# Row steps moved from VectorE to GpSimd, gate split moved to ScalarE and GpSimd, an early exp table, 65-column AV matmuls and a new order of the attention steps

## The chip, the cores and the metric

The kernel runs on one core of a Trainium2 chip. The metric is the device time of one execution in microseconds; the time of a kernel is the median of its runs.

## The reference

Attention over four batches with eight heads, 768 tokens and 64 dimensions, in which a query sees only the keys that were given the same of 16 centroids; then a layer of eight experts in which each token goes to one expert, by a greedy choice over all logits with a capacity of 384 tokens.

```python
q_assign = np.argmax(np.einsum('bhsd,hcd->bhsc', q_n, c_n), axis=-1)
k_assign = np.argmax(np.einsum('bhsd,hcd->bhsc', k_n, c_n), axis=-1)
mask = q_assign[:, :, :, None] == k_assign[:, :, None, :]
scores = scale * np.matmul(q, k.transpose(0, 1, 3, 2))
scores = np.where(mask, scores, -1000000000.0)
scores = scores - np.max(scores, axis=-1, keepdims=True)
attn = np.exp(scores)
attn = attn / (np.sum(attn, axis=-1, keepdims=True) + 1e-09)
out = np.matmul(attn, v)
...
for e in range(E):
    h = np.maximum(x[mask_e] @ w1[e], 0.0)
    out[mask_e] = h @ w2[e]
```

## The kernel before

**Units.** The attention is cut into eight units u (a batch and one half of its heads: four heads). Of each head there are six blocks of 128 queries and six of 128 keys. All operands are split into a high and a low f16 part, so that products are close to f32.

**Steps of a unit.** The kernel is written as named steps, and the string `ATT_ORDER` lists all of them in one order for the whole attention; the listed order is the program order on every engine, and no scheduler changes it. `load` brings q, k or v in, `split_sc`, `split_hi` (ScalarE) and `split_lo` (GpSimd for units 0 and 1, VectorE else) make the parts, `trans` or `pt`/`ptc` turn them around, `cent` and `hot0` to `hot5` find the centroid of each token. Then, 24 times each per unit:

- `m_mm` (TensorE, L765) computes the masked scores of one query block against all keys, and `m_rd` (VectorE, L769) takes the row maximum from PSUM;
- `b_mm` (TensorE, L804 and L808) computes the scores turned around, with the row maximum as additional rows of the operand, and `b_exp` (ScalarE, L811) the exponential;
- `res` (GpSimd, L819, tile `rt`; 12 of the 192 on VectorE) makes the low part of the exponential;
- `av` (TensorE, L830 to L836) multiplies with v: for each of six query blocks three matmuls, with 66, 64 and 66 columns, into the accumulator `av` in PSUM; one `av` in six has six more of 66 columns.

After the six `av` of a head, `out0`, `out1`, `out2`, `hi0` and `hi1` divide by the sum and split the result.

**Row steps.** When the 12 maxima of one half of a unit are there (six, one head, in unit 0), `row0` (L787) and `row1` (L783) make two small f16 tables from them on VectorE. `rowt` and `row2` are two DMAs on SyncE's queue that bring these tables into `qbt`, which the `b_mm` of that half read. `m_mm` of a later unit are listed between, so that TensorE has other work until then. `m_mm` and `b_mm` share three PSUM tiles `sc`.

**Around it.** `wgs` (`gate_split`, L547 and L548) splits the gate's weights on VectorE. The matmuls that form the logits (`lg0`) read them. `wd` (`dummy`, L655) is a matmul of 384 columns whose result nobody reads; there are 91, all in the first 46 us. `c1` takes square roots on ScalarE, and `b_exp` exponentials; ScalarE loads a table of functions before the first of each. `tab` steps fill tables that the second part needs. The second part, from 400 us on, is the routing and the experts (`FFN_ORDER`).

Of the kernel before, what the change touches and what calls it, by code (L numbers as in the profile page):

```python
# [25 lines left out]
hh3,0 hh4,0,k hh4,0,q split_sc,0,q,1 split_hi,0,q,1,P split_lo,0,q,1,P pt,0,qa,1 load,0,k,1 split_sc,0,k,1 split_hi,0,k,1,P
split_lo,0,k,1,P pt,0,ka,1 ptc,0,ka,1,D wd load,0,q,3 split_sc,0,q,3 split_hi,0,q,3,P split_lo,0,q,3,P load,0,k,3
split_sc,0,k,3 load,0,k,2 split_sc,0,k,2 wd wd wd wd load,0,v,- wd wd hh5,0,k split_sc,0,v,- wd wd zqb tab,4 cent0,1,k
ptc,0,qa,1,D ptc,0,qa,2,D tab,7 hh5,0,q cent0,1,q hh0,1 hh1,1 tab,2 pt,0,qa,3 pt,0,kb,0 split_hi,0,v,-,P ptc,0,kb,0,D
pt,0,qb,0 ptc,0,qb,0,A ptc,0,qa,3,D wd wd split_hi,0,k,3,P dup,0,k,3 hh2,1 hh3,1 wd dup,0,q,1 hh4,1,q load,1,v,- hh4,1,k  # L30
dup,0,k,1 hh5,1,q hh5,1,k wd wd wd wd tab,22 wd m_mm,0,1 m_rd,0,1 m_mm,0,0 wd wd wd wd wd split_hi,0,k,2,P dup,0,k,2
m_rd,0,0 m_mm,0,2 m_rd,0,2 wd wd pt,0,qb,1 ptc,0,qb,1,D dup,0,q,2 m_mm,0,4 m_rd,0,4 split_lo,0,v,-,P vs,0 split_lo,0,k,3,P
load,1,k,- split_sc,1,k,- pt,0,ka,3 ptc,0,ka,3,D split_lo,0,k,2,P pt,0,ka,2 tab,24 vh2,0 vact,0 tab,5 ptc,0,ka,2,A vl2,0
m_mm,0,5 m_rd,0,5 split_hi,1,k,-,P wd wd wd pt,0,kb,1 cent0,2,k cent0,2,q hh0,2 hh1,2 hh2,2 tab,8 hh3,2 hh4,2,q hh4,2,k wd
wd wd wd wd wd wd wd m_mm,0,3 m_rd,0,3 wd wd wd wd tab,23 ptc,0,kb,1,A m_mm,0,6 m_rd,0,6 cent0,3,k cent0,3,q hh0,3 row1,0,0
hh1,3 hh2,3 load,1,q,- wd row0,0,0 hh5,2,q tab,20 wd m_mm,0,8 pt,0,qb,2 wd wd dup,0,q,3 hh3,3 m_rd,0,8 m_mm,0,7 hh5,2,k
hh4,3,k hh4,3,q split_sc,1,q,- split_hi,1,q,-,P split_lo,1,k,-,P wd wd wd wd wd wd wd ptc,0,qb,2,A wd trans,1,ka,- m_rd,0,7
m_mm,0,10 m_rd,0,10 hh5,3,q hh5,3,k split_sc,1,v,- split_hi,1,v,-,P wd wd wd wd wd wd pt,0,kb,3 ptc,0,kb,3,D pt,0,kb,2
dup,1,k,- m_mm,0,11 wd ptc,0,kb,2,D wd wd m_mm,0,9 m_rd,0,11 cent,1,k,0 cent,1,k,3 cent,1,k,1 cent,1,k,2 split_lo,1,q,-,P
m_rd,0,9 hot0,1,k hot1,1,k pt,0,qm,0 row0,0,1 hot2,1,k ptc,0,qm,0,A pt,0,qb,3 ptc,0,qb,3,A m_mm,0,15 tab,34 m_rd,0,15  # L40
hot3,1,k row1,0,1 wd wd trans,1,qa,- wd b_mm,0,0 wd b_exp,0,0 res,0,0,P dup,1,q,- wd wd m_mm,0,12 hot4,1,k hot5,1,k
m_rd,0,12 wd wd m_mm,0,13 m_rd,0,13 m_mm,0,14 m_rd,0,14 cent,1,q,0 cent,1,q,3 cent,1,q,1 cent,1,q,2 hot0,1,q hot1,1,q
load,2,k,- pt,0,qm,1 trans,1,kb,- ptc,0,qm,1,A hot2,1,q wd wd split_lo,1,v,-,P b_mm,0,1 b_exp,0,1 res,0,1,P b_mm,0,2
b_exp,0,2 b_mm,0,3 wd wd wd hot3,1,q hot4,1,q b_exp,0,3 res,0,3,P m_mm,0,17 m_rd,0,17 m_mm,0,16 m_rd,0,16 tab,1 wd tab,16
hot5,1,q trans,1,qb,- m_mm,0,18 split_hi,2,k,-,D av,0,0 tab,17 row0,0,2 dup,2,k,- m_mm,0,22 row1,0,2 m_rd,0,18 vs,1
m_rd,0,22 tab,27 pt,0,qm,2 ptc,0,qm,2,A m_mm,0,19 vact,1 av,0,1 b_mm,0,4 m_rd,0,19 res,0,2,P b_exp,0,4 res,0,4,P b_mm,0,5
b_exp,0,5 split_lo,2,k,-,D tab,25 vh2,1 res,0,5,P load,2,q,- b_mm,0,6 b_exp,0,6 res,0,6,P vl2,1 m_mm,0,20 m_rd,0,20 tab,14
av,0,2 b_mm,0,7 b_exp,0,7 m_mm,0,21 m_rd,0,21 av,0,3 m_mm,1,0 m_rd,1,0 b_mm,0,9 b_exp,0,9 res,0,9,P m_mm,0,23 m_rd,0,23
row1,0,3 av,0,4 loadg row0,0,3 m_mm,1,1 m_rd,1,1 b_mm,0,8 b_exp,0,8 m_mm,1,2 m_rd,1,2 av,0,5 pt,0,qm,3 load,3,q,-
ptc,0,qm,3,A tab,30 res,0,8,P out0,0,0 b_mm,0,10 b_exp,0,10 wgs out1,0,0 out2,0,0,D m_mm,1,3 hi0,0,0 m_rd,1,3 b_mm,0,12  # L50
b_exp,0,12 b_mm,0,11 b_exp,0,11 m_mm,1,4 hi1,0,0 m_rd,1,4 split_hi,2,q,-,D av,0,6 m_mm,1,5 m_rd,1,5 b_mm,0,13 b_exp,0,13
res,0,7,P tab,6 av,0,7 av,0,8 split_lo,2,q,-,D res,0,10,P b_mm,0,14 b_exp,0,14 load,2,v,- m_mm,1,7 m_rd,1,7 m_mm,1,6
m_rd,1,6 res,0,11,P av,0,9 load,3,k,- av,0,10 m_mm,1,13 m_rd,1,13 split_hi,2,v,-,D res,0,13,P av,0,11 out0,0,1 res,0,12,P
out1,0,1 out2,0,1,D b_mm,0,15 m_mm,1,8 m_rd,1,8 m_mm,1,11 m_rd,1,11 trans,2,ka,- tab,21 cent,2,k,0 cent,2,k,1 cent,2,k,2
b_exp,0,15 trans,2,qa,- m_mm,1,10 m_rd,1,10 hi0,0,1 res,0,14,P hi1,0,1 b_mm,0,17 b_exp,0,17 cent,2,k,3 hot0,2,k res,0,15,P
b_mm,0,18 hot1,2,k m_mm,1,9 res,0,17,P m_rd,1,9 tab,3 tab,32 row1,1,0 b_exp,0,18 b_mm,0,16 b_exp,0,16 xst,0,0 row0,1,0
tab,26 av,0,12 av,0,13 av,0,14 hot2,2,k hot3,2,k split_hi,3,k,-,D split_lo,3,k,-,D b_mm,0,19 b_exp,0,19 b_mm,0,20 hot4,2,k
av,0,15 b_exp,0,20 hot5,2,k res,0,16,P av,0,16 av,0,17 out0,0,2 m_mm,1,14 m_rd,1,14 b_mm,0,21 b_exp,0,21 out1,0,2 out2,0,2,D
b_mm,0,22 b_exp,0,22 xtr,0,0 lg0,0,0 lg1,0,0 res,0,18,P m_mm,1,12 m_rd,1,12 hi0,0,2 res,0,19,P hi1,0,2 b_mm,0,23 m_mm,1,18
cent,2,q,0 m_rd,1,18 b_exp,0,23 cent,2,q,3 m_mm,1,15 m_rd,1,15 res,0,22,P rowt,1,0 res,0,20,P row2,1,0 b_mm,1,1 b_exp,1,1  # L60
m_mm,1,19 trans,2,kb,- cent,2,q,2 dup,2,q,- split_hi,3,q,-,D cent,2,q,1 m_mm,1,16 m_rd,1,19 m_rd,1,16 m_mm,1,17 hot0,2,q
m_rd,1,17 av,0,18 b_mm,1,3 av,0,19 res,0,23,P b_mm,1,2 b_exp,1,3 b_exp,1,2 hot1,2,q b_mm,1,0 av,0,20 b_exp,1,0 hot2,2,q
hot3,2,q hot4,2,q hot5,2,q trans,3,ka,- res,0,21,P av,0,21 res,1,1,P b_mm,1,5 b_exp,1,5 res,1,5,P m_mm,1,21 load,4,q,-
split_lo,2,v,-,D m_rd,1,21 av,0,22 av,0,23 out0,0,3 tab,36 m_mm,1,20 res,1,2,P m_rd,1,20 b_mm,1,6 b_exp,1,6 out1,0,3
out2,0,3,D hi0,0,3 m_mm,1,23 trans,2,qb,- vs,2 vact,2 res,1,0,P m_mm,1,22 b_mm,1,4 b_exp,1,4 m_rd,1,23 res,1,4,P b_mm,1,7
b_exp,1,7 hi1,0,3 m_rd,1,22 row1,1,1 av,1,0 res,1,3,P b_mm,1,8 b_exp,1,8 row0,1,1 rowt,1,1 vh2,2 m_mm,2,1 av,1,1
split_lo,3,q,-,D m_rd,2,1 m_mm,2,3 av,1,2 vl2,2 m_mm,2,0 xst,0,1 b_mm,1,10 b_exp,1,10 av,1,3 m_rd,2,3 av,1,4 res,1,6,P
load,3,v,- m_rd,2,0 row2,1,1 m_mm,2,2 m_rd,2,2 av,1,5 out0,1,0 tab,18 res,1,8,P cent,3,k,0 out1,1,0 out2,1,0,D m_mm,2,4
b_mm,1,11 m_rd,2,4 b_exp,1,11 m_mm,2,5 cent,3,k,2 xtr,0,1 res,1,10,P hi0,1,0 m_rd,2,5 hi1,1,0 cent,3,k,1 cent,3,k,3
res,1,7,P hot0,3,k hot1,3,k b_mm,1,9 b_exp,1,9 res,1,9,P m_mm,2,7 m_rd,2,7 m_mm,2,8 load,4,k,- tab,28 m_rd,2,8 av,1,6  # L70
b_mm,1,12 tab,10 b_exp,1,12 av,1,7 res,1,11,P av,1,8 av,1,9 hot2,3,k hot3,3,k dup,3,k,- b_mm,1,14 b_exp,1,14 hot4,3,k
hot5,3,k res,1,12,P res,1,14,P tab,33 av,1,10 av,1,11 trans,3,qa,- b_mm,1,13 m_mm,2,6 out0,1,1 out1,1,1 b_exp,1,13
res,1,13,P out2,1,1,D hi0,1,1 m_rd,2,6 b_mm,1,17 b_exp,1,17 res,1,17,P b_mm,1,15 b_exp,1,15 hi1,1,1 xtr,1,0 lg0,0,1 lg1,0,1
lg2,0,1 m_mm,2,9 m_rd,2,9 m_mm,2,14 m_rd,2,14 b_mm,1,16 load,4,v,- m_mm,2,11 m_rd,2,11 av,1,12 res,1,15,P b_exp,1,16
m_mm,2,10 xst,1,0 m_rd,2,10 av,1,13 m_mm,2,13 m_rd,2,13 m_mm,2,12 m_rd,2,12 row1,2,0 row0,2,0 rowt,2,0 av,1,14
# [1394 lines left out]
```

## Time and profile before

| | us |
|---|---|
| median of 3 runs (lowest to highest) | 704.22 (703.09 to 706.07) |
| the profiled execution | 704.8 |
| its span, first to last instruction | 703.0 |
| TensorE busy in the span | 659.1 |
| VectorE busy | 522.7 |
| GpSimd busy | 497.2 |
| ScalarE busy | 424.0 |
| mean granted clock of TensorE | 0.968 |

Matmuls are pipelined: a busy time of TensorE holds the latency of each, so that what it could take is read from the distance between starts. The attention lies in the first 400 us. The share of an engine is read there by stretches, not over the whole span.

### The profile page before, as it was taken

Reading aid. Unit: us, or ns where it says so; the run is one execution under the profiler, and the core shown is the slowest. Engines: PE = TensorE matmul, PEld = TensorE weight load, DVE = VectorE, ACT = ScalarE, POOL = GpSimd, SP = SyncE. Lnnn points to the kernel's source line nnn. Section 1 sums busy time; section 2 is a strip of 40 time slices with the busy share of each in tenths; the row PEclk is TensorE's granted clock in tenths of the full one; section 3 lists DMA queues with packets and bytes.
Section 4 is the critical chain, followed back from the end, with each engine's and each line's share of the span. In section 5 each row is a group of like instructions: output and inputs, shape, how many; then the busy total and the mean of one; then the engine's idle time right before and its main releaser. Section 6 shows DMA issues by size and latency. Waiting matters only on the chain. (4 is left out here: it accounts for less than half of the span.)

```text
span 703.0 us, 19737 instructions
## 1 busy us (share of the span) xinstructions
PE 659.1 (94%) x8274; PEld 438.3 (62%) x8274; DVE 522.7 (74%) x1149; ACT 424.0 (60%) x554; POOL 497.2 (71%) x395
## 2 busy tenths in 40 slices
PE   7988999969999999999998778999999999999996
...
DVE  6999989998899999987887867868676666742020
...
PEclk9999999998999999999999958999999999999998
...
GB/s 199 124 181 221 94 182 183 173 171 115 109 192 183 155 121 167 119 82 120 62 35 48 70 24 263 137 195 277 108 320 106 284 134 242 173 324 238 37 9 45
DMA packets 175450, 105.84 MB, mean 151 GB/s; under 512 B 135426, under 2 KB 160002, under 8 KB 175362
## 3 DMA queue, kind: packets, MB, share of 16 engines
...
q14 instruction: 24, 0.20, 0.1%
HBM read 58.77 MB, written 12.58 MB: 101 GB/s over the span
## 5 line engine op out<-in xcount | busy, mean ns | idle before, releaser
L819 POOL TENSOR_TENSOR rt<-pt 128x768 f16<-128x768 f32 x180 | 277.7, 1569 | 74.6 <-ACT pt L811 70.4
L811 ACT ACTIVATE pt<-sc 128x768 f32<-128x768 f32 x192 | 150.9, 811 | 114.3 <-PE sc L808 99.2
L769 DVE TENSOR_REDUCE mxs<-sc 128x1 f32<-128x768 f32 x192 | 177.0, 949 | 19.9 <-PE sc L765 18.8
L1392 PE MATMUL pf<-xgt,w1h 128*128 128x384 f16 (+1 forms) x640 | 129.0, 293 | 0.2 <-DVE xgt L729 0.2
L830 PE MATMUL av<-vh,pt 128*128 128x66 f16 x1152 | 123.5, 195 | 3.5 <-DVE xb L863 3.5
L833 PE MATMUL av<-vh,rt 128*128 128x66 f16 x1152 | 123.2, 195 | 0.6 <-POOL rt L819 0.6
L832 PE MATMUL av<-vl,pt 128*128 128x64 f16 x1152 | 123.2, 193 | 0.0
L832 PEld LDWEIGHTS <-pt 128*128 128x128 bf16 x1152 | 107.3, 99 | 11.3 <-issue 4.6
L830 PEld LDWEIGHTS <-pt 128*128 128x128 bf16 x1152 | 107.8, 99 | 8.9 <-DVE xb L863 1.0
L833 PEld LDWEIGHTS <-rt 128*128 128x128 f16 x1152 | 106.8, 98 | 0.7 <-POOL rt L819 0.7
L765 PE MATMUL sc<-kbt,qbt 80*128 80x384 f16 x384 | 91.8, 330 | 11.0 <-DVE mxs L769 9.1
L804 PE MATMUL sc<-qbt,kbt 99*128 99x384 f16 x384 | 95.4, 329 | 3.3 <-DVE mxs L769 1.8
L808 PE MATMUL sc<-qat,kat 128*128 128x384 f16 x384 | 95.5, 330 | 0.0
L1392 PE MATMUL pf<-xgt,w1l 128*128 128x384 f16 (+1 forms) x320 | 90.0, 294 | 0.0
L1354 ACT ACTIVATE wr<-wr 128x1024 f32<-128x1024 f32 x64 | 66.7, 1046 | 24.6 <-DMA wr<-in_moe_w_dram 24.6
L1392 PEld LDWEIGHTS <-w1h 128*128 128x128 f16 x640 | 57.2, 97 | 29.1 <-issue 1.5
L1430 PE MATMUL pf<-w2h,hh 128*128 128x512 f16 x192 | 72.7, 378 | 0.0
L1430 PE MATMUL pf<-w2h,hl 128*128 128x512 f16 x192 | 72.6, 378 | 0.0
L1430 PE MATMUL pf<-w2l,hh 128*128 128x512 f16 x192 | 72.6, 378 | 0.0
L1368 POOL DMA_INDIRECT xg<-xrow,idx x24 | 23.3, 969 | 65.3 <-DVE idx L1327 33.8
L1364 POOL TENSOR_TENSOR w2l<-wr,w2h 128x1024 f16<-128x1024 f32 x32 | 67.7, 2136 | 1.4 <-ACT w2h L1357 1.0
L1364 POOL TENSOR_TENSOR w1l<-wr,w1h 128x1024 f16<-128x1024 f32 x32 | 67.3, 2130 | 0.2
...
## 6 DMA issues: line engine op xcount, KB each, us to landing
...
xg<-xrow,idx POOLq DMA_INDIRECT x24, 6.2
```

Of the source, the lines that this page charges most:

```text
L765: nc.tensor.matmul(p[:, half, :S // 2], QBT[u][:D + C, i, :], KBT[u][:D + C, h * J + half * 3:h * J + half * 3 + 3, :], start=True, stop=True)
L769: nc.vector.tensor_reduce(mxs[u % 3][:, i:i + 1], MP.pop((u, i))[:, :, :S // 2], axis=AX.XY, op=OP.max)
L804: nc.tensor.matmul(ps[:, half, :S // 2], KBT[u][:ER + 3, s, :], QBT[u][:ER + 3, cs, :], start=True, stop=False)
L808: nc.tensor.matmul(ps[:, half, :S // 2], KAT[u][:, s, :], QAT[u][:, cs, :], start=False, stop=True)
L811: nc.scalar.activation(pts[(u * 12 + s // 2) % RP][:, s % 2], MP.pop((u, "b", s))[:, :, :S // 2], AF.Exp, scale=ESC)
L819: (nc.vector if e == "D" else nc.gpsimd).tensor_sub(rts[x][:, s % 2], p.rearrange("p a b -> p (a b)"), hi_view(pts[x])[:, s % 2])
L830: nc.tensor.matmul(o[:, j, :], hi[:, js], VH[u][:, s, :], start=(kt == 0 and j == 0), stop=False, skip_group_check=True)
L832: nc.tensor.matmul(o[:, j, :D], hi[:, js], VL[u][:, s, :], start=False, stop=False, skip_group_check=True)
L833: nc.tensor.matmul(o[:, j, :], r[:, js], VH[u][:, s, :], start=False, stop=(kt == J - 1), skip_group_check=True)
L1364: nc.gpsimd.tensor_sub(lo, wrs[c], hi)
L1392: nc.tensor.matmul(o, (w1l if i == 2 else w1h)[x][:, c, fs], xgt[x][:, h + int(i == 1), ts], start=(first and i == 0), stop=(last and i == ...
L1430: nc.tensor.matmul(PS["o", p, g], (hl if i == 2 else hh)[x][:, f, g * P:(g + 1) * P], (w2l if i == 1 else w2h)[x][:, f, :], start=(f == 0 ...
```

## The change

`row0` and `row1` run on GpSimd. The gate split becomes three steps: `wg0` and `wg1` scale and round on ScalarE, `wg2` subtracts on GpSimd. A new step `et` takes one exponential right after the square root, so that the second table is loaded at the start. The accumulator `av` is one tile that is made once; the matmuls into it write 65 columns in place of 66 (the 66th was never read). `ATT_ORDER` lists the steps in another order, with 12 `wd` in place of 91; otherwise it holds the same steps, each on the same engine. `FFN_ORDER` is unchanged.

```diff
+    avb = pav.tile([P, 512], F32, name="av")
+    AW = J * (D + 2)
+    def acc():
+        return avb[:, :AW].rearrange("p (j d) -> p j d", d=D + 2)
...
-    def gate_split():
-        nc.vector.tensor_scalar(wg[:, :, 0, :], wgf, SX, None, op0=OP.mult)
-        nc.vector.scalar_tensor_tensor(wg[:, :, 1, :], wgf, SX, wg[:, :, 0, :], op0=OP.mult, op1=OP.subtract)
+    def gate_sc():
+        nc.scalar.activation(wgf, wgf, AF.Copy, scale=SX)
+    def gate_hi():
+        nc.scalar.activation(wg[:, :, 0, :], wgf, AF.Copy)
+    def gate_lo():
+        nc.gpsimd.tensor_sub(wg[:, :, 1, :], wgf, wg[:, :, 0, :])
+    def table():
+        nc.scalar.activation(etl, ss[:, 0:1], AF.Exp, scale=0.0)
...
     def row0(u, g):
         e, m, cs = rows(u, g)
-        nc.vector.tensor_scalar(m, twice(u, cs), -(2.0 ** 29), -1.0 / BIG, op0=OP.max, op1=OP.mult)
+        nc.gpsimd.tensor_scalar(m, twice(u, cs), -(2.0 ** 29), -1.0 / BIG, op0=OP.max, op1=OP.mult)
     def row1(u, g):
         e, m, cs = rows(u, g)
-        nc.vector.tensor_scalar(e, twice(u, cs), -(2.0 ** 29), None, op0=OP.is_lt)
+        nc.gpsimd.tensor_scalar(e, twice(u, cs), -(2.0 ** 29), None, op0=OP.is_lt)
...
-            AV[u, h] = pav.tile([P, J, D + 2], F32, name="av")
+            AV[u, h] = acc()
...
-            nc.tensor.matmul(o[:, j, :], hi[:, js], VH[u][:, s, :], start=(kt == 0 and j == 0), stop=False,
+            nc.tensor.matmul(o[:, j, :D + 1], hi[:, js], VH[u][:, s, :D + 1], start=(kt == 0 and j == 0), stop=False,
...
-misc load,0,k,0 wtio wd loadc c0 c1 c2,0 c2,1 zkb split_sc,0,k,0 split_hi,0,k,0,P split_lo,0,k,0,P dup,0,k,0 load,0,q,0
+loadc ident c0 c1 c2,0 c2,1 misc wtio c2,2 c2,3 wd wd c2,4 zqb c2,5 zkb et c2,6 c2,7 c2,8 c2,9 load,0,q,0 c2,10 c2,11 c2,12
```

Three places show what the new order does.

VectorE in unit 2, at the row steps of its second half (L787 is `row0`, L783 `row1`, L769 `m_rd`, L634 `split_lo` of a later q), before:

```order
L769 TENSOR_REDUCE mxs_142<-sc 128x1
L863 TENSOR_TENSOR xb_145<-av,xb_145 128x6x64
L769 TENSOR_REDUCE mxs_142<-sc 128x1 x2
L787 TENSOR_SCALAR m_94<-mxs_142 128x12x2
L634 SCALAR_TENSOR_TENSOR qa<-ld_76,qa 128x24x64
L783 TENSOR_SCALAR m_94<-mxs_142 128x12x2
L769 TENSOR_REDUCE mxs_140<-sc 128x1 x5
```

GpSimd at the same row steps after (L831 is `res`, L799 `row1`, L795 `row0`, L949 a table's fill; the numbers of tiles differ between the two programs):

```order
L831 TENSOR_TENSOR rt_136<-pt_132 128x768
L831 TENSOR_TENSOR rt_133<-pt_129 128x768
L949 MEMSET wdig_161 128x128
L831 TENSOR_TENSOR rt_135<-pt_131 128x768
L831 TENSOR_TENSOR rt_133<-pt_129 128x768
L799 TENSOR_SCALAR m_96<-mxs_144 128x12x2
L795 TENSOR_SCALAR m_96<-mxs_144 128x12x2
L831 TENSOR_TENSOR rt_134<-pt_130 128x768 x2
```

The row steps left VectorE's row of maxima and stand between the residues of GpSimd.

VectorE at the gate split in unit 0 before (L547 and L548 are the split, L840, L843, L851 and L863 the steps `out0`, `out1`, `out2`, `hi1`, L769 `m_rd`):

```order
L769 TENSOR_REDUCE mxs_141<-sc 128x1 x2
L840 TENSOR_SCALAR rc<-av 128x6
L547 TENSOR_SCALAR wg<-wgf 128x4x8
L548 SCALAR_TENSOR_TENSOR wg<-wgf,wg 128x4x8
L843 RECIPROCAL rc<-rc 128x6
L851 TENSOR_TENSOR av<-av,rc 128x6x64
L769 TENSOR_REDUCE mxs_141<-sc 128x1
```

ScalarE at the gate split in unit 0 after (L551 and L554 are `wg0` and `wg1`, L823 `b_exp`, L641 `split_hi`, L696 `hot5`, L739 `ptc`):

```order
L641 ACTIVATE qa<-ld_79 128x24x64
L696 ACTIVATE qb<-ceq 128x24x16
L823 ACTIVATE pt_129<-sc 128x768
L551 ACTIVATE wgf<-wgf 128x32
L554 ACTIVATE wg<-wgf 128x4x8
L641 ACTIVATE ka<-ld_78 128x24x64
L739 ACTIVATE qbt_120<-sc 3x768
```

The split no longer stands between the two steps that divide a head's result; its last step stands on GpSimd, eight rows of `res` and tables later.

ScalarE at the start of the program before (L516 is `c1`, L625 `split_sc`, L629 `split_hi`, L643 and L641 `dup`):

```order
L516 ACT_TABLE_LOAD
L516 ACTIVATE ss<-ss 128x1
L625 ACTIVATE ld_75<-ld_75 128x384
L629 ACTIVATE ka<-ld_75 128x6x64
L643 ACTIVATE kb<-ka 128x6x64
L625 ACTIVATE ld_76<-ld_76 128x384
L629 ACTIVATE qa<-ld_76 128x6x64
```

And after (L520 is `c1`, L560 `et`, L637 `split_sc`, L641 `split_hi`, L653 `dup`):

```order
L520 ACT_TABLE_LOAD
L520 ACTIVATE ss<-ss 128x1
L560 ACT_TABLE_LOAD
L560 ACTIVATE etl<-ss 128x1
L637 ACTIVATE ld_77<-ld_77 128x384
L637 ACTIVATE ld_76<-ld_76 128x384
L641 ACTIVATE ka<-ld_76 128x6x64
```

The second table load moved ahead of the first split; before it stood in front of the first `b_exp`.

## Rows read from the trace of the kernel before

**Rows 1.** The page: busy time of TensorE (microseconds, share, instructions), and the span in 40 slices of 17.6 us, the busy share of each engine in tenths and the granted clock.

```profile
PE 659.1 (94%) x8274; PEld 438.3 (62%) x8274; DVE 522.7 (74%) x1149; ACT 424.0 (60%) x554; POOL 497.2 (71%) x395
PE   7988999969999999999998778999999999999996
DVE  6999989998899999987887867868676666742020
PEclk9999999998999999999999958999999999999998
```

**Rows 2.** The span in stretches of 100 us: length, busy time and instructions of PE, PEld, DVE, ACT and POOL, granted clock, share and rate of the DMA engines.

```profile
0.00:100.00 100.00, 87.55 (x1201) 62.47 (x1202) 86.07 (x162) 73.15 (x101) 67.55 (x77) 0.97 0.72 169
100.00:200.00 100.00, 92.66 (x1513) 68.73 (x1511) 91.65 (x135) 59.57 (x78) 81.81 (x58) 0.95 0.71 154
200.00:300.00 100.00, 96.49 (x1689) 73.05 (x1687) 95.00 (x141) 67.83 (x85) 83.69 (x56) 1.00 0.73 152
300.00:400.00 100.00, 94.39 (x1672) 71.44 (x1669) 80.02 (x136) 52.53 (x75) 74.34 (x54) 1.00 0.33 67
```

**Rows 3.** Who waited for whom: total microseconds, times, longest.

```profile
ACT pt L811 <- PE sc L808: 99.2, 94, 11.0
...
PE sc L765 <- DVE mxs L769: 9.1, 4, 5.0
```

**Rows 4.** The timeline of all engines around 147 us, at the row steps of unit 2: start, duration, engine, line, operation, count, idle time before it and who ended it.

```profile
146.82 7.15 POOL L819 TENSOR_TENSOR rt<-pt 128x768 f16<-128x768 f32 x5
146.97 7.10 DVE L787 TENSOR_SCALAR m<-mxs 128x24 f16<-128x24 f32 x1
...
156.68 0.80 PE L765 MATMUL sc<-kbt,qbt 80*128 80x384 f16 x2 [5.05 <-DVE mxs L769]
```

**Rows 5.** The same timeline around 61 us, at the gate split.

```profile
59.66 4.39 POOL L819 TENSOR_TENSOR rt<-pt 128x768 f16<-128x768 f32 x3
...
61.15 1.43 DVE L547 TENSOR_SCALAR wg<-wgf 128x32 f16<-128x32 f32 x1
...
62.62 1.48 DVE L548 SCALAR_TENSOR_TENSOR wg<-wgf,wg 128x32 f16<-128x32 f32 x1
...
65.71 0.48 PE L765 MATMUL sc<-kbt,qbt 80*128 80x384 f16 x2 [2.34 <-DVE mxs L769]
```

**Rows 6.** Two short stretches in the columns of Rows 2; the granted clock is the third number from the end.

```profile
67.00:71.00 4.00, 4.00 (x51) 3.13 (x49) 2.92 (x4) 1.91 (x2) 2.97 (x2) 0.57 0.01 4
...
156.00:163.00 7.00, 6.26 (x50) 3.88 (x50) 5.50 (x9) 0.81 (x1) 0.43 (x1) 0.51 0.66 149
```

**Rows 7.** Row steps on VectorE by group: count, busy microseconds, mean nanoseconds, idle time before.

```profile
L787 DVE TENSOR_SCALAR m<-mxs 128x24 f16<-128x24 f32 x14 | 13.0, 926 | 0.1
...
L783 DVE TENSOR_SCALAR m<-mxs 128x24 f16<-128x24 f32 x14 | 5.7, 407 | 0.2
...
L783 DVE TENSOR_SCALAR qm<-mxs 128x12 f16<-128x12 f32 x4 | 2.4, 590 | 0.0
...
L787 DVE TENSOR_SCALAR qm<-mxs 128x12 f16<-128x12 f32 x4 | 1.6, 410 | 0.0
```

**Rows 8.** The instructions of single lines: count, shortest, median and longest duration in nanoseconds, first and last start (L787 `row0`, L783 `row1`).

```profile
L787 DVE TENSOR_SCALAR m<-mxs x14: 214/228/7097, 80.3 to 367.7; 128x24 f16<-128x24 f32 x14
L783 DVE TENSOR_SCALAR m<-mxs x14: 213/226/1483, 80.4 to 368.0; 128x24 f16<-128x24 f32 x14
```

**Rows 9.** The same columns: `split_lo` of k on VectorE, which stays there.

```profile
L634 DVE SCALAR_TENSOR_TENSOR ka<-ld,ka x6: 1740/1782/3021, 51.8 to 259.3; 128x1536 f16<-128x1536 f32 x6
```

**Rows 10.** The timeline near the end of the attention: two `res` on VectorE, and the TensorE instruction that next waits for VectorE.

```profile
371.77 5.50 DVE L819 TENSOR_TENSOR rt<-pt 128x768 f16<-128x768 f32 x2 [3.60 <-ACT pt L811]
...
379.33 0.19 PE L830 MATMUL av<-vh,pt 128*128 128x66 f16 x1 [2.32 <-DVE xb L863]
```

**Rows 11.** The timeline of TensorE at full clock: first matmul of an `av` and the first instruction behind its 18; then the first of 12 matmuls of `lg0` and the two pairs of 384 columns behind them.

```profile
302.55 0.19 PE L830 MATMUL av<-vh,pt 128*128 128x66 f16 x1
...
303.09 0.49 PE L765 MATMUL sc<-kbt,qbt 80*128 80x384 f16 x2
...
305.14 0.17 PE L891 MATMUL mx<-wg,xt 128*128 128x16 f16 x1
...
305.45 0.48 PE L804 MATMUL sc<-qbt,kbt 99*128 99x384 f16 x2
305.77 0.49 PE L808 MATMUL sc<-qat,kat 128*128 128x384 f16 x2
```

**Rows 12.** The dummies, in the columns of Rows 8.

```profile
L655 PE MATMUL av<-wt,onesh x91: 323/326/528, 4.9 to 45.8; 128*128 128x384 f16 x91
```

**Rows 13.** The group of `res` on GpSimd, in the columns of Rows 7, and the only small operation with a scalar that GpSimd has, in those of Rows 8.

```profile
L819 POOL TENSOR_TENSOR rt<-pt 128x768 f16<-128x768 f32 x180 | 277.7, 1569 | 74.6 <-ACT pt L811 70.4 <-PE sc L765 3.7
...
L575 POOL TENSOR_SCALAR vm<-vm,rest x3: 273/273/278, 2.1 to 4.0; 2x8 f16<-2x8 f16 x3
```

**Rows 14.** The two DMAs of a row chain on SyncE's queue, in the columns of Rows 8, and the time from issue to landing of the first.

```profile
L790 SPq DMA_TRANSPOSE mt<-m x14: 1110/1130/1645, 81.9 to 368.5; - x14
L794 SPq DMA_DIRECT2D qbt<-mt x14: 762/796/928, 86.8 to 371.2; - x14
...
DMA to landing us min/median/max: 3.2/3.6/4.0
```

**Rows 15.** The timeline of ScalarE at the first exponential.

```profile
37.64 1.28 ACT L811 ACT_TABLE_LOAD   x1
```

More of the change, by code (lines that the diff above doesn't have):

```diff
@@ L26 @@
[L26 to L75, printed above, removed]
@@ new lines @@
+cent,1,k,3 hot0,1,k m_mm,0,13 split_hi,1,v,-,P split_lo,1,v,-,P b_mm,0,1 b_exp,0,1 m_rd,0,13 hot1,1,k res,0,1,P wd pt,0,kb,3
+wd ptc,0,kb,3,D load,3,k,- pt,0,qb,3 ptc,0,qb,3,A m_mm,0,17 m_rd,0,17 b_mm,0,0 b_exp,0,0 hot2,1,k m_mm,0,15 m_rd,0,15
+b_mm,0,4 b_exp,0,4 res,0,4,P b_mm,0,3 b_exp,0,3 m_mm,0,16 load,2,q,- b_mm,0,5 b_exp,0,5 hot3,1,k hot4,1,k hot5,1,k
+cent,1,q,0 m_rd,0,16 m_mm,0,9 m_rd,0,9 dup,1,k,- res,0,0,P row0,0,1 cent,1,q,3 row1,0,1 cent,1,q,2 cent,1,q,1 hot0,1,q
+res,0,3,P m_mm,0,14 m_rd,0,14 b_mm,0,2 b_exp,0,2 m_mm,0,12 av,0,0 m_rd,0,12 hot1,1,q pt,0,qm,1 ptc,0,qm,1,A m_mm,0,20
```

265 lines of the change are left out of this document (154 added, 111 removed).

## Prediction

> **What bounds the kernel now.** I read the page first [rows 1]. TensorE shows 9 tenths in most slices, but VectorE shows 8 or 9 tenths from the second slice to the seventeenth: in the attention two engines are full at once. The stretches say where [rows 2]: VectorE is busy for 86, 92 and 95 of the first three hundreds of microseconds and for 80 of the fourth. Next to it I put TensorE's own need. At full clock the 18 matmuls of an `av` take from 302.55 to 303.09, 0.54 us or 30.0 ns each, and a pair of 384 columns takes 0.32 us [rows 11]. With `m_mm` one pair, `b_mm` two and `av` 18 matmuls, one of the 192 steps costs TensorE 0.32 + 0.64 + 0.54 = 1.5 us, all of them 288 us; centroids, transposes, logits and the value sums add some 35 by the same pace (my estimate). So TensorE could do the attention in about 325 us and takes 400. Third, the waits [rows 3]. ScalarE's 99 us behind `b_mm` is harmless, since it is the engine with the most room. The row that costs is the small one: TensorE waited four times, 9.1 us in all, for a row maximum on VectorE. The timeline names what held VectorE up. At 146.97 a `row0` on 24 elements takes 7.10 us, next to five `res` on GpSimd that run back to back from 146.82 for 7.15 us, and TensorE then stands still for 5.05 us [rows 4]. At 61.15 the two instructions of the gate split take 2.9 us beside three `res`, and TensorE waits 2.34 us [rows 5]. The median `row0` takes 0.23 us [rows 8]. So a small VectorE operation from SBUF to SBUF can be held until GpSimd pauses, and the maxima queue behind it. Fourth, the clock: in 156 to 163, right after the 5.05 us, the granted clock is 0.51, the lower level, and in 67 to 71, after the 2.34 us, 0.57 [rows 6].
>
> The Trainium skill, "SBUF — State Buffer", section "SBUF: two separate sides", says that VectorE and GpSimd share a port pair as an exclusive lock that the first one holds for its whole instruction. The trace agrees that the one shuts the other out, but the 7.10 us cover five instructions, not one. By the page alone `row0` would have lost one `res` at most, some 1.5 us, and the sum below would be about 8 us smaller; the row decides.
>
> **The change part by part.** The sum is made against the profiled execution's 704.8 us (span 703.0 and 1.8 around it), 0.6 above the median.
>
> *Waits that go: -9.1 us.* The row steps and the gate split leave VectorE. Of the 9.1 us, 5.05 and 2.34 are theirs by the timeline [rows 3 to 5]; I give them the rest too, since several `row1` and `row0` also stretched (one `row1` to 1.48 us [rows 8]).
>
> *Clock that comes back: -5.1 us.* At half the pace 7 us at 0.51 lose 3.4 us, and 4 us at 0.57 lose 1.7 [rows 6]. The gaps before them go, so the drops should.
>
> *VectorE time that shows in no gap: -4 us.* The row steps take 13.0 + 5.7 + 2.4 + 1.6 = 22.7 us of VectorE [rows 7], the gate split 2.9. At the median the 36 would take about 7, so that some 15 is being held up. Before 160 us VectorE is the fuller engine; from the same rows some 16 us of these lie there, and 7.4 are already counted as gaps. Of the 8.4 left I take about half, the rest going under where TensorE is last: bounds 0 and -8.4.
>
> *The row steps on GpSimd: 0.* The trace has no such operation there; the nearest are 0.27 us for a scalar operation on 2 by 8 elements and 1.57 us for a `res` on 768 [rows 13]. With 24 elements I take the lower, 36 x 0.27 = 10 us on an engine that is busy for 307 of the first 400 us [rows 2]. What is queued behind a row step on GpSimd is the next `res`, and `av` waits for that; but the new order puts the row steps behind `res` that follow the last maximum, so that they should find it done. The upper end, 1.57 each, is 57 us and would still fit in the 92 idle ones. Their chain goes on through two DMAs on SyncE, 1.13 to issue and 3.6 to land, then 0.80 and a landing, about 7 us [rows 14]. By the order, with the durations above, TensorE has 8.3 us of work between the last maximum of unit 1's first half and the `b_mm` that needs it (9.5 before), 7.3 in unit 2 (9.0 before), and 12 to 17 in units 3 to 6 (7 to 12 before). So the early chains are as tight as before and the late ones looser. I put +1 us for new small waits.
>
> *Dummies and start: +2 us.* 79 dummies of 0.16 us are 12.8 us of TensorE, by their count [rows 12] and the pace of a matmul of 384 columns [rows 11], but all lie before 46 us, where VectorE is the full engine and loads set the pace; in the slots they fill TensorE waits anyway, so I give nothing for them. They also keep the clock up. Without them TensorE has by the order some 16 us of work before the first `b_mm`, in about 37 us, and may be at the lower level. Its matmul pair then takes 0.65 us, still less than the 0.9 of a maximum. The exponential's table, 1.28 us [rows 15], moves to the start, in front of the first split on ScalarE: it delays the first maxima by that much and is given back at the first exponential. Bounds: -3, if the dummies did stand in the way, and +8, if the clock stays low through unit 0.
>
> *65 columns: -1 us.* From 384 columns (0.32 / 2 = 160 ns) to 65.3 on average (30.0 ns) one column is worth 130 / 319 = 0.41 ns; 2 x 1152 + 192 = 2496 matmuls lose a column, 1.0 us. Twelve matmuls of 16 and 8 columns take 0.31 us, 25.8 ns each [rows 11], so that at 66 columns the pace is still set by columns. Bounds: 0, if something else sets it, and -1.0. The Trainium skill, "TensorE: Matmul & The Clock Gate", section "Back-to-back issue gap", gives about 81 ns for pairs of weight load and matmul at 128 columns, with the load as a part; by that the narrower matmul would gain nothing and the sum would be 1 us higher. No run here has 128 columns in such a stream, and the 30.0 ns speak for the column.
>
> *What stays.* The larger VectorE operations with two inputs from SBUF stay beside GpSimd: `split_lo`, once 3.02 us where the shortest is 1.74 [rows 9], and the two `res` at 371.77 that took 5.50 us and cost TensorE 2.32 us [rows 10].
>
> Sum: -9.1 - 5.1 - 4 + 1 + 2 - 1 = -16.2, so 688.6 for the profiled execution and **688.0 us** for the median. A second way agrees roughly: by the order, VectorE has 76 us of work up to the last `av` of unit 0 in place of 81 and 6 of stalls, which is 11 less; half of this is lost at the start, where it waits for ScalarE's splits.
>
> **The rivals.**
>
> *The stalls move.* GpSimd stays as full, and VectorE's splits and `res` still meet it; with the row steps away the next such meeting is late instead. For it: [rows 9, 10]. Against it: in this trace the splits lost at most 1.3 us, and no more than two of the four gaps stand near one. If half of the 14.2 us of gaps and clock comes back: 704.2 - 9 = 695.
>
> *More comes off.* If the whole 8.4 us of VectorE's hidden time is on the path and the start gains 3: 688 - 4.4 - 5 = 679.
>
> *Nothing comes of it.* The row steps on GpSimd come late behind `res` runs, so that each of the 14 chains of units 1 to 7 makes TensorE wait. It cancels the gain at 16 / 14 = 1.2 us a chain, which is the spare time of the two tightest (8.3 and 7.3 against 7). For it: those two. Against it: the ten later ones have 5 us to spare. Time: 704.
>
> *Slower, by the clock.* With the dummies gone TensorE sits at the lower level through unit 0. One step then takes it 3.0 us against 76 / 24 = 3.2 of VectorE, so that it stays hidden if all is even, and binds wherever work bunches. Each 2 us of TensorE-bound time at half clock cost 1 us; the gain of 18 is gone after 36 us of it, and 60 us would give 716. For it: the page's clock falls after pauses of 2 to 5 us, and the new start is full of them. Against it: the falls that are seen last 3.4 us at 0.5 once TensorE is busy (7 x 0.49, 4 x 0.43).
>
> **How the numbers follow.** The forecast gets 0.53, moved stalls 0.20, more 0.14, nothing 0.07, slower 0.06. The range reaches from 679 to 700: the upper end covers moved stalls with 5 us more, and half of the case that more comes off, all of the nothing case and the slower one are left out, 0.20. About 0.5% is what a measurement of this kernel can tell from no change. Faster by that is below 700.7: forecast, moved stalls and more, 0.87; within, 0.07; slower, 0.06.
>
> **What would show it.** Right: no VectorE row of 24 elements; TensorE's waits for `m_rd` well under 9.1 us; granted clock 1.00 in the stretch of unit 2; row steps on GpSimd near 0.3 us; `av` at 29.6 ns; the last `av` near 380 in place of 396. Wrong: a clock near 0.5 in the first 60 us with TensorE busy; waits of `b_mm` for `qbt`'s DMA; `res` waiting behind a row step; or a start that is later by more than 3 us.

## The result, and the profile after

The changed kernel takes **685.62 us** (median of 4 runs, 684.39 to 686.45) against 703.65 us for the kernel before in the same comparison. The ratio is 0.9745, interval 0.9702 to 0.9787: about 18 us less. The forecast was 688.0, range 679 to 700. The profiled execution has a span of 683.4 us in place of 703.0. All of the difference arises in the attention: the last `av` starts at 376.6 us where it started at 396.1, and from there to the end the kernels take 306.8 and 306.9 us.

The page of the kernel after, busy time of TensorE and the span in 40 slices, to be read beside [rows 1]:

```profile
PE 640.7 (94%) x8195; PEld 427.7 (63%) x8195; DVE 503.3 (74%) x1111; ACT 421.9 (62%) x557; POOL 500.6 (73%) x432
...
PE   4699999999999999999999779999999999999996
...
DVE  6999999999889988877667667877767575832020
...
PEclk9899999999999999999999669999999999999998
```

The stretches of 100 us, the two short ones, and one of the start, in the columns of [rows 2, 6]:

```profile
0.00:100.00 100.00, 81.53 (x1220) 59.69 (x1221) 92.22 (x156) 77.58 (x112) 76.43 (x87) 0.97 0.77 187
100.00:200.00 100.00, 95.81 (x1666) 72.10 (x1664) 93.50 (x142) 65.86 (x84) 88.02 (x75) 1.00 0.80 160
200.00:300.00 100.00, 98.90 (x1750) 75.15 (x1749) 91.10 (x139) 64.61 (x85) 85.61 (x69) 1.00 0.71 142
...
67.00:71.00 4.00, 3.98 (x65) 2.90 (x64) 3.90 (x7) 2.22 (x4) 2.59 (x2) 1.00 1.21 252
156.00:163.00 7.00, 6.89 (x122) 5.15 (x122) 6.43 (x14) 4.04 (x6) 7.00 (x6) 1.00 0.38 82
...
20.00:40.00 20.00, 13.88 (x181) 9.58 (x180) 19.62 (x32) 15.48 (x22) 10.10 (x8) 0.83 0.62 144
```

Between 100 and 300 us the clock is full throughout, and TensorE is busy for 95.8 and 98.9 of each hundred where it was 92.7 and 96.5. GpSimd went up, from 81.8 and 83.7 to 88.0 and 85.6. One stretch got worse: in 20 to 40 us the granted clock is 0.83 where the kernel before has 1.00; it holds 6.8 us at the lower level.

Who waits for whom on TensorE, the answer to [rows 3]:

```profile
PE sc L816 <- DMA qbt<-mt: 2.8, 4, 1.0
...
PE sc L777 <- DVE mxs L781: 1.7, 2, 1.0
```

The waits of the next `m_mm` for a maximum fell from 9.1 us to 1.7, the longest from 5.0 to 1.0. The row chain's last DMA is now the longer wait.

The row steps (L795 is `row0`, L799 `row1`) by line, as in [rows 8], and one pair in its place on GpSimd's timeline, the second half of unit 2:

```profile
L795 POOL TENSOR_SCALAR m<-mxs x14: 375/382/393, 76.3 to 350.3; 128x24 f16<-128x24 f32 x14
...
L799 POOL TENSOR_SCALAR m<-mxs x14: 351/362/1792, 76.1 to 350.0; 128x24 f16<-128x24 f32 x14
```

```profile
135.22 4.32 POOL L831 TENSOR_TENSOR rt<-pt 128x768 f16<-128x768 f32 x2 [1.17 <-ACT pt L823]
139.51 0.35 POOL L799 TENSOR_SCALAR m<-mxs 128x24 f16<-128x24 f32 x1
139.74 0.38 POOL L795 TENSOR_SCALAR m<-mxs 128x24 f16<-128x24 f32 x1
140.00 4.31 POOL L831 TENSOR_TENSOR rt<-pt 128x768 f16<-128x768 f32 x3
```

There is no idle time in brackets at these row steps: when GpSimd comes to them, the maxima are there.

### The profile page after: what moved, and what is told of

The parts are those of the page before. It is cut to its first block, busy times and chain, and to the rows that moved or that the text cites. A ratio compares the mean times of both kernels' runs of the same rounds, so it can differ in the third digit from the quotient of the medians.

```text
span 683.4 us, 19589 instructions
## 1 busy us (share of the span) xinstructions
PE 640.7 (94%) x8195; PEld 427.7 (63%) x8195; DVE 503.3 (74%) x1111; ACT 421.9 (62%) x557; POOL 500.6 (73%) x432
## 5 line engine op out<-in xcount | busy, mean ns | idle before, releaser
L831 POOL TENSOR_TENSOR rt<-pt 128x768 f16<-128x768 f32 x180 | 271.3, 1529 | 47.7 <-ACT pt L823 45.1
L823 ACT ACTIVATE pt<-sc 128x768 f32<-128x768 f32 x192 | 150.5, 811 | 92.8 <-PE sc L820 70.4
L781 DVE TENSOR_REDUCE mxs<-sc 128x1 f32<-128x768 f32 x192 | 179.2, 963 | 24.6 <-PE sc L777 23.4
L842 PE MATMUL av<-vh,pt 128*128 128x65 f16 x1152 | 119.4, 194 | 1.0 <-DVE xb L875 1.0
L845 PE MATMUL av<-vh,rt 128*128 128x65 f16 x1152 | 119.3, 193 | 0.0
L844 PE MATMUL av<-vl,pt 128*128 128x64 f16 x1152 | 119.2, 191 | 0.0
L844 PEld LDWEIGHTS <-pt 128*128 128x128 bf16 x1152 | 105.7, 98 | 8.3 <-issue 2.1
L842 PEld LDWEIGHTS <-pt 128*128 128x128 bf16 x1152 | 106.1, 97 | 6.5
L845 PEld LDWEIGHTS <-rt 128*128 128x128 f16 x1152 | 105.3, 97 | 0.0
L816 PE MATMUL sc<-qbt,kbt 99*128 99x384 f16 x384 | 93.7, 325 | 4.0 <-DMA qbt<-mt 2.8
L820 PE MATMUL sc<-qat,kat 128*128 128x384 f16 x384 | 93.7, 325 | 0.0
L777 PE MATMUL sc<-kbt,qbt 80*128 80x384 f16 x384 | 88.5, 326 | 3.8 <-DVE mxs L781 1.7
```

The lines of the kernel that those rows point to most:

```text
L777: nc.tensor.matmul(p[:, half, :S // 2], QBT[u][:D + C, i, :], KBT[u][:D + C, h * J + half * 3:h * J + half * 3 + 3, :], start=True, stop=True)
L781: nc.vector.tensor_reduce(mxs[u % 3][:, i:i + 1], MP.pop((u, i))[:, :, :S // 2], axis=AX.XY, op=OP.max)
L816: nc.tensor.matmul(ps[:, half, :S // 2], KBT[u][:ER + 3, s, :], QBT[u][:ER + 3, cs, :], start=True, stop=False)
L820: nc.tensor.matmul(ps[:, half, :S // 2], KAT[u][:, s, :], QAT[u][:, cs, :], start=False, stop=True)
L823: nc.scalar.activation(pts[(u * 12 + s // 2) % RP][:, s % 2], MP.pop((u, "b", s))[:, :, :S // 2], AF.Exp, scale=ESC)
L831: (nc.vector if e == "D" else nc.gpsimd).tensor_sub(rts[x][:, s % 2], p.rearrange("p a b -> p (a b)"), hi_view(pts[x])[:, s % 2])
```

## The experiments

Ratios are to the kernel before, run on the same chip. A price "above after" is the difference of the ratio to 0.9745, times 703 us. The kernel after was not run beside these, so that such a price carries both intervals: 3 us each way from the kernel after, and another 1.5 to 3 from the run.

### The four corners

**Row steps back on VectorE, in the new order:**

```diff
-        nc.gpsimd.tensor_scalar(m, twice(u, cs), ...)   # row0, and row1 alike
+        nc.vector.tensor_scalar(m, twice(u, cs), ...)
```

> The kernel after, with nothing changed but the engine of the row steps: row0 and row1 are on VectorE again, at their places in the new order. Theory (the row steps are what GpSimd holds up): several of the 14 row0 take well over 1 us beside res on GpSimd, TensorE again waits for maxima, and the time rises by 6 to 13 us, to 692 to 699; it need not be all of the 12.5 us that the prediction gave the row steps (its 9.1 + 5.1 + 4 less the gate split's 4.0, less 1.7 that may be hidden), since the new order asks for them at other moments. Rival (the new order did it): the row steps still stretch, but nothing waits for them where they now stand; 685 to 688.

Measured: 704.15 us, ratio 1.0017 (0.9995 to 1.0039). The whole gain is gone, 19.1 us above after. The rival, that the new order did it, falls; the theory had the direction, and its 6 to 13 us were too few. The groups of VectorE (busy time, mean) and the timeline of GpSimd and VectorE around 77 us:

```profile
L799 DVE TENSOR_SCALAR m<-mxs 128x24 f16<-128x24 f32 x14 | 10.6, 760 | 0.2
...
L795 DVE TENSOR_SCALAR m<-mxs 128x24 f16<-128x24 f32 x14 | 8.2, 586 | 0.2
```

```profile
74.57 7.16 POOL L831 TENSOR_TENSOR rt<-pt 128x768 f16<-128x768 f32 x5
...
77.71 1.25 DVE L799 TENSOR_SCALAR m<-mxs 128x24 f16<-128x24 f32 x1
78.83 1.55 DVE L795 TENSOR_SCALAR m<-mxs 128x24 f16<-128x24 f32 x1
```

The row steps are held here too, but by the rest of one `res` or little more: the longest takes 2.14 us, the rest of one and the whole of the next, and the longest wait of TensorE behind a pair is 2.5 us (an `av` that waits for `hi1`, right behind these two) in place of the 5.05 of [rows 4]. With the eight instructions of unit 0 they make 20.8 us of VectorE, and the kernel is 19.1 us longer. The two profiles differ in the clock too: before the last `av` this one has 10.2 us more at the lower level. Of these 6.8 lie ahead of the first `av`, which starts 1.6 us later; the other 3.4 are worth up to 1.7 at half pace.

**Row steps on GpSimd, in the old order,** alone and with the other parts of the change. The second run has 12 dummies, every eighth of the old ones; its accumulator `av` is still made anew for each head. Its other edits are left out here:

```diff
-        nc.vector.tensor_scalar(m, twice(u, cs), ...)   # before.row0, and row1 alike
+        nc.gpsimd.tensor_scalar(m, twice(u, cs), ...)
```

> The kernel before, with nothing changed but the engine of the row steps: row0 and row1 on GpSimd, at their old places. Theory (row steps held on VectorE): the 5.05 us wait and the half clock behind it go, and the time falls by 6 to 12 us, to 692 to 698. Rival (the order did it): at their old places the row steps stand on GpSimd behind res that have not yet run, the row chains come late, TensorE waits for the second DMA of the chain at b_mm in place of the maxima; 700 to 708.

> The kernel before with every part of the change but the order: row steps on GpSimd, gate split on ScalarE and GpSimd, 65 columns, the early exponential table, and 12 of the 91 dummies, all at the old places. Theory (engines, not the order): 686 to 692, within 6 us of the kernel after. Rival (the order carries the gain): 694 or more, since the old order puts the row steps behind waiting res on GpSimd.

Measured: 716.6 us, ratio 1.0208 (1.0174 to 1.0243), for the row steps alone; 715.91 us, 1.0182 (1.0138 to 1.0226), for the other parts with them. Both are *slower* than before, by some 13 to 15 us, and both times the rival is right, more strongly than it said. Who waits for whom with the row steps alone, first GpSimd, then TensorE:

```profile
POOL m L783 <- DVE mxs L769: 12.3, 5, 3.2
...
POOL qm L787 <- DVE mxs L769: 6.4, 1, 6.4
...
POOL m L787 <- DVE mxs L769: 3.7, 3, 2.2
```

```profile
PE av L833 <- POOL rt L819: 8.3, 8, 2.1
...
PE sc L804 <- DMA qbt<-mt: 4.4, 4, 1.9
```

At the old places the row steps stand on GpSimd where their maxima are not ready. GpSimd waits for them 22.4 us, the `res` queued behind wait with it, and TensorE waits 8.3 us for `res` (0.6 before) and 4.4 us for row chains. In the kernel after the same three rows of GpSimd's waits add up to 5.1 us, 3.6 of them in the start.

So the corners are:

| ratio to before | old places | new places |
|---|---|---|
| row steps on VectorE | 1 | 1.0017 |
| row steps on GpSimd | 1.0208 alone, 1.0182 with the rest | 0.9745 |

Neither half gives anything without the other. The column of the new places holds the gate split, the table, the 65 columns and the 12 dummies too; that they do not bring the gain without the order is shown by the 1.0182, and what each is worth in the new order was not run, the dummies apart.

### What holds VectorE

**Row steps in the accumulating form, in the old order, on VectorE:**

```diff
-        nc.vector.tensor_scalar(m, twice(u, cs), -(2.0 ** 29), -1.0 / BIG, op0=OP.max, op1=OP.mult)
+        nc.vector.tensor_scalar(w, twice(u, cs), -(2.0 ** 29), None, op0=OP.max, op1=OP.max, accum_out=ra[:, 0:1])
+        nc.vector.tensor_scalar(m, w, -1.0 / BIG, None, op0=OP.mult, op1=OP.max, accum_out=ra[:, 1:2])
...                              # row1 alike, one instruction
```

> The kernel before, row steps left on VectorE at their old places, but written in the form that also writes out its accumulator (a maximum over the row that nobody reads); row0's two operations become two such instructions, since this form has one operation. This asks why VectorE is held at all. The Trainium skill, SBUF - State Buffer, section Who interferes with whom, says that tensor_scalar takes the port pair shared with GpSimd by running in a two-port mode, and that the form with an accumulator does not. Theory by that page: no row step over 0.4 us beside res, the 5.05 us wait goes, and the time falls by 5 to 11 us, to 693 to 699, though VectorE runs 36 more instructions of some 0.25 us each (my estimate from the 0.23 us of a row0). Rival (any VectorE instruction from SBUF to SBUF is held): the 7.10 us row0 is there again, and with more instructions the time is 704 to 710.

Measured: 698.12 us, ratio 0.994 (0.9918 to 0.9963): 4.2 us less, inside the theory's range of times and just short of its 5 us. None of the 108 instructions (54 and the reads of the accumulator) is held; the longest takes 0.275 us. But the gap did not go. The timelines of GpSimd, VectorE and TensorE, at the place of [rows 4]:

```profile
142.56 7.15 POOL L823 TENSOR_TENSOR rt<-pt 128x768 f16<-128x768 f32 x5
```

```profile
142.71 0.27 DVE L791 TENSOR_SCALAR_CACHE_REDUCE m<-mxs 128x24 f16<-128x24 f32 x1
...
142.82 8.52 DVE L636 SCALAR_TENSOR_TENSOR qa<-ld,qa 128x1536 f16<-128x1536 f32 x1
```

```profile
152.57 1.66 PE L767 MATMUL sc<-kbt,qbt 80*128 80x384 f16 x4 [4.80 <-DVE mxs L771]
```

`row1` passes in 0.27 us beside the same run of five `res`. The next VectorE instruction, `split_lo` with two inputs from SBUF, takes 8.52 us in place of 1.75: it starts 0.26 us into the run and ends 1.6 us behind its end, and TensorE waits 4.80 us. The hold moved, as the prediction's first rival says, and it moved to the instruction that the prediction named under "what stays".

**The gate split alone, in the old order:**

```diff
-wgs
+wg0 wg1 wg2
```

> The kernel before with the gate split alone changed: a scaling and a copy on ScalarE and a subtraction on GpSimd, all three where the two VectorE instructions stood. Theory (the prediction's terms): the 2.34 us gap at 65.71 and the 1.7 us of half clock behind it go, 4.0 us less, 698 to 701. Rival (the hold moves): in the same stretch of back-to-back res the next VectorE instruction that needs the port, split_hi or split_lo of q, is held in its place; 701 to 703.

Measured: 700.99 us, ratio 0.9982 (0.9961 to 1.0003): 1.3 us less, not clear of nothing, and not the 4.0 of the theory. The wait did go, from 9.1 us of waits for maxima to 6.8, but the rival's mark is there too: the next `split_lo` on VectorE takes 2.96 us in place of 1.75. The row of `row0` shows why the rest is as before:

```profile
PE sc L770 <- DVE mxs L774: 6.8, 4, 4.8
...
66.20 2.96 DVE L639 SCALAR_TENSOR_TENSOR qa<-ld,qa 128x1536 f16<-128x1536 f32 x1
...
L792 DVE TENSOR_SCALAR m<-mxs x14: 217/229/7097, 77.7 to 361.9; 128x24 f16<-128x24 f32 x14
```

**The accumulating form in the new order:**

```diff
-        nc.gpsimd.tensor_scalar(m, twice(u, cs), ...)
+        (the two instructions above, and one for row1, on VectorE)
```

> The kernel after with the row steps on VectorE in the accumulating form that was not held in the old order (row0 as two instructions), and nothing on GpSimd for them. With the plain row steps on VectorE this order took 704.2 us. Theory A (there VectorE was the full engine, and both the time that the row steps need and the time that they are held lie on its path): of the 20 us some 12 were holds and these go, while the work stays and grows a little; 691 to 698. Theory B (holds alone): 685 to 689, as on GpSimd. Theory C (the hold moves to split_lo, as it did in the old order): 698 to 704, with split_lo well over 3 us.

Measured: 699.71 us, ratio 0.9953 (0.9925 to 0.9982), 14.6 us above after. Theory A missed its range by 2 us, B is out. C has the number, but its mark is absent: the longest `split_lo` takes 3.03 us, as in the kernel after. The row steps' records add up to 18.4 us here, none of them held (longest 0.268 us); they overlap, and VectorE is busy with them for 10.8 us. The stretch from the first `av` to the last, in the columns of [rows 2], in the kernel after, with the plain row steps on VectorE, and with these:

```profile
46.20:376.60 330.40, 321.32 (x5560) 242.16 (x5558) 290.17 (x445) 213.16 (x281) 278.64 (x230) 1.00 0.67 138
...
47.80:394.20 346.40, 325.61 (x5558) 243.49 (x5557) 304.18 (x477) 213.53 (x281) 269.24 (x198) 1.00 0.65 131
...
47.90:389.40 341.50, 324.87 (x5557) 242.93 (x5556) 298.35 (x541) 213.32 (x281) 271.04 (x198) 1.00 0.66 133
```

VectorE is busy 14.0 and 8.2 us longer than in the kernel after, the stretch is 16.0 and 11.1 us longer, and VectorE's idle time stays at 40 to 43 us. So in the new order most of the time that VectorE gets is on the path, held or not. It is not all: TensorE's waits for row chains are 6.0 us here where the kernel after has 2.8.

### The price of a microsecond on each engine, in the new order

**Row steps issued two and four times on GpSimd:**

```diff
-        nc.gpsimd.tensor_scalar(m, ...)
+        for _ in range(4):        # 2 in the other run; row1 alike
+            nc.gpsimd.tensor_scalar(m, ...)
```

> The kernel after with every row step issued four times on GpSimd, the same values written again: 3 x 36 x 0.38 = 41 us more work on GpSimd, 1.1 us more in each row step, 2.2 in each chain. It prices the row steps where they now stand. Theory (GpSimd has room and the chains of the later units have time to spare, as the prediction says): only the chains that TensorE already waits for lose, four b_mm by 2.2 us each at most; 686 to 694. Rival (GpSimd is as full as it can be): half or more of the 41 us shows, over 705.

> The kernel after with every row step issued twice on GpSimd: 36 x 0.37 = 13.4 us more work there, in the same places as the four times of the run before, which cost 44 us for 40. Theory A (GpSimd's time is on the path at any amount in this order): a third of that, 698 to 702. Theory B (the order leaves room behind each row step, and only what goes past it counts): 685 to 691.

Measured: 729.35 us, ratio 1.0381 (1.0339 to 1.0423), for four times, 44.7 us above after for 45.9 us more of row steps (59.8 in place of 13.9); 691.03 us, 0.9826 (0.9795 to 0.9856), for two, 5.7 us above for 12.5 more. The rival was right for four times. Two times stops at the upper end of B: there is some room, and it ends inside the first dozen microseconds. Part of the price of four times is clock: in its first three hundreds of microseconds it was granted 0.93, 0.93 and 0.98, where the kernel after has 0.97, 1.00 and 1.00, which is worth up to some 13 of the 44.7 us (an estimate from these shares). With four times TensorE waits at:

```profile
PE av L847 <- POOL rt L833: 12.5, 12, 2.6
PE sc L818 <- DMA qbt<-mt: 9.5, 7, 2.7
```

**One more instruction on ScalarE behind each exponential:**

```diff
+        table()       # in b_exp: one column, nobody reads it
```

> The kernel after with one more instruction on ScalarE behind each of the 192 exponentials: an exponential of one column into a tile that nobody reads, by the 0.20 us of the one at the start 38 us more on ScalarE, about what the row steps four times over put on GpSimd. Theory A (ScalarE is the engine with the most room, as the prediction read its 99 us of waiting for b_mm): 685 to 695. Theory B (in this order every engine is on the path, whatever its busy share): 715 to 730.

Measured: 687.68 us, ratio 0.9773 (0.9746 to 0.9801), 2.0 us above after, within the intervals of no change. Theory A. The added group:

```profile
L560 ACT ACTIVATE etl<-ss 128x1 f32<-128x1 f32 x193 | 38.6, 200 | 0.0
```

**Dummies.** The kernel after with 91 and with none, the kernel before with 12:

```diff
-wd
+wd wd wd wd wd wd wd wd       # or nothing; seven or eight at each of the 12 places
```

> The kernel after with 91 dummies again, at the places where the 12 stand now, seven or eight at each. The prediction gave the missing dummies 2 us of loss by the clock, with bounds from -3 to +8. Theory (at the start loads, ScalarE and VectorE set the pace and not TensorE's clock): 684 to 687, though the granted clock in 27 to 34 us rises from 0.5. Rival A (the clock mattered): 680 to 683. Rival B (the dummies stand in the way): 688 to 694.

> The kernel after without its last 12 dummies. With 79 more, 12.6 us of TensorE at full clock, it took 9.5 us more. Theory A (a dummy stands in the way of what follows): 12 x 0.16 to 0.33 = 2 to 4 us less, 681.5 to 684, below both kernels. Theory B (the 12 that are left stand where TensorE waits anyway): 685 to 687. Theory C (they keep the clock up in the start): 688 or more, with the lower level before 60 us.

> The kernel before with 12 of its 91 dummies, every eighth left in its place, and nothing else changed. The prediction gave the missing 79 a loss of 2 us by the clock, bounds -3 to +8. Theory A (in the old order they fill waits): 701 to 705. Theory B (they stand in the way, as in the new order): 694 to 699. Theory C (the clock): 706 to 710, with the lower level in much of the first 60 us.

Measured: 695.13 us, ratio 0.989 (0.9862 to 0.9918), with 91 in the new order, 10.2 us above after: rival B by its direction, 1 us past its range. The first `av` starts at 52.5 us in place of 46.2. TensorE's timeline shows one such place, behind a pause, at half clock (0.32 us each):

```profile
31.92 0.47 PE L659 MATMUL mx<-ct,kat 128*128 128x16 f16 x12 [3.00 <-DVE ceq L692]
...
33.15 4.80 PE L666 MATMUL av<-wt,onesh 128*128 128x384 f16 x15
```

Without any: 688.09 us, 0.9781 (0.9756 to 0.9807), 2.5 us above; the interval overlaps that of the kernel after, so the last 12 can't be told from none. (Theory C's number and mark are there, with a granted clock of 0.66 in 20 to 40 us, but the first `av` starts at 46.3 us, no later.) Before with 12: 707.21 us, 1.0062 (1.004 to 1.0085), 4.4 us slower. It lies 2 us above A's range and inside C's, and C's mark shows in part: 10.2 of the first 60 us are at the lower level. Its stretch of 20 to 40 us, in the columns of [rows 2], against a granted clock of 1.00 in the kernel before:

```profile
20.00:40.00 20.00, 16.61 (x187) 11.87 (x187) 17.18 (x36) 16.02 (x22) 8.07 (x8) 0.80 0.60 112
```

In the old order, then, the dummies were worth something; in the new one, at the 12 places, they stand in the way.

## Why the prediction held, step by step

**Waits that go (-9.1).** The trace after says -7.4 (1.7 left). The step was right in kind and somewhat too large. What it leaves out is that leaving VectorE is only half the reason: in the old order the held instruction would have been replaced by the next one (`split_lo`, 8.52 us), or by a GpSimd that itself waits.

**Clock (-5.1).** Right in kind, too small. The kernel after has no stretch at the lower level (1.2 GHz) between 46 and 376 us; before there were four, of 3.4, 3.4, 6.8 and 3.4 us. At half the pace these 17.0 us are worth up to 8.5. I had counted the two that follow the large gaps. (The words on the rival "slower", that such a fall lasts 3.4 us, are wrong for the one of 6.8.) That a gap brings the fall is not shown for the smaller one: the run of before with 12 dummies has the same wait at the gate split, and full clock behind it:

```profile
67.17 0.49 PE L759 MATMUL sc<-kbt,qbt 80*128 80x384 f16 x2 [2.34 <-DVE mxs L763]
...
67.00:75.00 8.00, 7.83 (x142) 5.96 (x142) 7.61 (x12) 5.85 (x7) 6.13 (x5) 1.00 0.52 106
```

And one sign that the prediction gave for being wrong did come: a clock near 0.5 in the start, from 27 to 34 us. It did no harm there, as the first `av` starts no later than before.

**VectorE's hidden time (-4, bounds 0 and -8.4).** Most likely the term that was too small; by itself it was not measured. With the waits and the clock it gave the row steps 12.5 us, as the expectation of the run with them on VectorE counts, and that run says 19.1. In the new order their time on VectorE shows nearly whole: 20.8 us cost 19.1, gaps and clock included, and 10.8 us without a hold cost 14.6. That half of it goes under where TensorE is last was a guess, and the runs are against it.

**Row steps on GpSimd (0).** No run takes the row steps off both engines, so that the 0 is not measured by itself. The reason given for it holds at the new places: GpSimd finds the maxima done, but for 1.5 us of waits in units 1 to 7. I took 0.27 us for a step and it is 0.36 to 0.38, once 1.79. At the old places the same step costs 14.6 us. And the sentence that 57 us would still fit into GpSimd's 92 idle ones is wrong: 12.5 us more cost 5.7, and 45.9 cost 44.7. The idle share said nothing on room. My reading, which no run tests, is that much of it is waiting for exponentials (45.1 us in the kernel after) whose `res` TensorE then needs soon.

**New waits (+1).** `b_mm` waits 2.8 us for row chains where the trace of before has 1.5: right.

**Dummies and start (+2).** The first `av` of unit 0 starts at 46.2 us in place of 46.3, so the start came out even, 2 us better than the term. By themselves the missing dummies cost 4.4 us in the old order, inside the bounds of -3 and +8; in the new order the start does without them.

**65 columns (-1).** This gave nothing. The 18 matmuls of an `av` span the same 0.54 us as in [rows 11]; the first and the one behind them, on TensorE's timeline after:

```profile
202.03 0.20 PE L842 MATMUL av<-vh,pt 128*128 128x65 f16 x1
...
202.57 0.49 PE L816 MATMUL sc<-qbt,kbt 99*128 99x384 f16 x2
```

A column is not what sets 30.0 ns at this size. By the Trainium skill, "TensorE: Matmul & The Clock Gate", section "Back-to-back issue gap", the spacing in a stream of weight loads and matmuls is set by both of a pair. The trace agrees in that the column gained nothing, though at 30.0 ns and far from the 81 that the Trainium skill gives there for 128 columns; no run here shows that weight loads are what sets it.

**The sum** of -16.2 against some -18 is right by terms that err in both directions, so that its closeness is in part luck; its mechanism, small VectorE operations held by `res`, is shown. What it could not see is how much hung on the order: the case "slower" got 0.06, as a clock effect, while the same engines in the old order gave +13 to +15 us, by a mechanism I had put under "nothing comes of it" at 0.07 (row steps late behind or in front of `res`).

**What is left of the rival "the stalls move".** One such meeting is in the kernel after: a `tab` step (L942), a one-input operation from SBUF to SBUF on VectorE. Timelines of VectorE, GpSimd and TensorE:

```profile
168.29 3.52 DVE L942 TENSOR_SCALAR sel<-sel 128x128 f16<-128x128 f16 x1
168.60 3.21 DVE L781 TENSOR_REDUCE mxs<-sc 128x1 f32<-128x768 f32 x1
```

```profile
168.87 2.88 POOL L831 TENSOR_TENSOR rt<-pt 128x768 f16<-128x768 f32 x2
```

```profile
171.91 0.27 PE L758 MATMUL mx<-vh,onesh 128*128 128x256 f16 x1 [1.41 <-DVE rc L852]
```

It ends with the second `res`, and TensorE waits 1.41 us. Placing it elsewhere was not tried. No version tried beats the kernel after.

**Open.** That VectorE is the full engine of the new order is read from prices, from its idle time that stays the same, and from its 91 to 94 busy microseconds of 100; why the new order with VectorE's row steps comes out just even with the old one was not taken apart further. The order's own parts were not separated, nor the gate split, the early table and the columns in the new order.
